# Order of the first operands, unordered scatters, and where the early units' weights lie

## The chip, the cores and the metric

The kernel runs on one core of a Trainium2 chip. The metric is the time of one execution on the device, in microseconds. The core has five engines that run side by side, each through its own instructions in order: TensorE (PE; its weight loads are PEld), VectorE (DVE), ScalarE (ACT), GpSimd (POOL) and SyncE (SP), which here only issues DMAs and loads registers. Sixteen DMA engines move data between the device's memory and the on-chip memory; transfers whose rows are picked by an index list are issued by POOL, nearly all others by SP.

## What is computed

Three layers, all in float32 at the edges. The attention has 4 x 8 heads of 576 positions and 64 columns, with a decay from the running sum of log f:

```python
log_f = np.log(np.clip(f, 0.0001, 1.0)); cum = np.cumsum(log_f, axis=-1)
scores = scale * q @ k.T + cum[:, :, :, None] - cum[:, :, None, :]     # causal
attn_out = softmax(scores) @ v                                         # (4, 8, 576, 64)
x = attn_out.transpose(0, 2, 1, 3).reshape(2304, 512)
# mixture: each token goes to one of 8 experts
logits = x @ w_gate + modality_bias[modality_id]; e = argmax(logits)
x = gate * (relu(x @ w1[e]) @ w2[e])                                   # w1 512x1024, w2 1024x512
# second layer: a rational function between two products
h = x @ w_in; g = P(h) / (Q(h) + 1e-6); out = g @ w_out                # 512x2048, 2048x512
```

## The kernel before, in words

The program is not issued as it is written. `Rec` records every operation with its engine, a cost, the operations that it depends on, a priority (`up`, plus an offset by kind) and extra order edges (`order`); `flush` (line 230) then lists all of them through a model of the engines and issues each engine's instructions in the order found. So nearly every instruction in the profile has line 163, and tiles tell the stages apart. Some order is written by hand: while `line` is set, SP's transfers keep their written order; while `chained` is set, TensorE's do; `gate` holds back all that follows behind one operation.

**Start.** `constants` and `masks` fill constants and the causal masks; `Attention.setup` (line 587) zeroes the operand tiles of all pairs of heads ("ka", "qa", "one" on POOL; "hq", "lq" on DVE) and makes the decay's running sums, which go through memory ("cums") into rows of "ka". Then pairs 0 and 1 are transposed and split into high and low parts (`parts`), pair 0's row maxima are taken (`maxes`, `turned`), the router is set up (`Route.setup`), and the scales of V are computed (`scales`) and applied (`vparts`, on POOL).

**Attention.** 16 pairs of heads, software-pipelined by the string ORDER: in the loop of pair p, TensorE makes maxima for p+1 (M), scores for p (S), values for p-1 (V), router logits for p-2 (L) and transposes for p+2 (T). An exponential leaves ACT in a tile of the ring "pe" (four), ACT casts it to 16 bits, and POOL subtracts to get the low part "lo". "pe" and "lo" lie in the memory "old"; raw Q, K, V and the value scales' input lie in "prep".

**Routing.** After every fourth pair a batch of 576 tokens is routed (`Route.batch`, line 982): the token numbers and gates of each expert are scattered into a table in memory, with five transfers of up to 128 rows. `Route.early` picks two full blocks of 128 tokens from the first two batches; `Route.final` (line 1070) lays out all others after the fourth.

**Units.** A unit is one expert for one block of 128 tokens, or two blocks ("double"). `fetch` (line 1228) reads its part of the table and gathers the tokens; `pieces` (line 1201) brings the expert's weights in 16 pieces of 256 KB, each cast (ACT) and subtracted (DVE) into two parts, through rings of 4 raw and 3 converted tiles. There are two early units, then eight double and seven single ones. The rings lie in the memory of "old", which the program takes over when the attention has left it (`Mixed`), and all eight PSUM banks are likewise taken over after the attention (`banks_of`); an early unit uses four of them, two for products with w1 ("ph") and two for products with w2 ("py").

**Second layer.** `Weights.fill` (line 1151) converts 32 tiles of w_in and w_out from float64 into the memories that the attention has left, gated behind the last of `final`. `Second.tile` (line 1381) then computes nine tiles of 256 tokens and scatters the output rows by token number, two transfers each; the list lays them among the remaining units.

What a scatter waits for is decided in two places: the recorder sees a write to the whole table, and the framework below it adds a wait behind the transfer before, in the table and in the output.

Of the kernel before, what the change touches and what calls it, by code (L numbers as in the profile page):

```python
# [11 lines left out]
P = 128  # L12
# [31 lines left out]
class Rec:  # L44
# [10 lines left out]
    def __init__(s, nc):  # L55
        s.nc, s.ops, s.acc, s.bank, s.up, s.tag, s.memory, s.order, s.pages = nc, [], {}, {}, 0, '', {}, [], {}
        s.chained, s.link = False, None
        s.line, s.tail, s.gate = False, None, None
        for e in s.ENG:
            setattr(s, e, Port(s, e))  # L60
# [65 lines left out]
    def op(s, e, cost, fn, ins=(), outs=(), deps=(), share=1.0):  # L126
# [103 lines left out]
    def flush(s):  # L230
# [31 lines left out]
        for t, i in best[1]:  # L262
            ops[i][2]()

# [282 lines left out]
class Attention:  # L547
# [13 lines left out]
    def __init__(s, nc, ar, f32r, prep, ya, old, banks, dr, q, k, v, f, c):  # L561
# [7 lines left out]
        s.pe, s.lo = old.ring(b["pe"], [P, 2, 512]), old.ring(b["hl"], [P, 2, 1664], F16)  # L569
# [17 lines left out]
    def setup(s, f32r):  # L587
# [6 lines left out]
        for t in s.ka.bufs:  # L594
# [9 lines left out]
        G.memset(s.one.bitcast(F32), 0.0)  # L604
        for h in range(2):
            G.memset(s.one[64 * h + 32:64 * h + 34].bitcast(F32), 1.0)
# [87 lines left out]
    def prep(s, p):  # L694
        s.load(p)
        s.loadv(p)
        s.sums(p)
        s.vparts(p)
# [92 lines left out]
    def scores(s, p, g):  # L791
# [63 lines left out]
class Route:  # L855
# [14 lines left out]
    def load(s):  # L870
# [7 lines left out]
        nc.sync.dma_start(out=s.table.rearrange("(p c) t -> p (c t)", p=P), in_=z)  # L878
# [103 lines left out]
    def batch(s, b):  # L982
# [37 lines left out]
        V.tensor_copy(row, r)  # L1020
        for c in range(NB):
            n = P if c < 4 else 64
            nc.gpsimd.indirect_dma_start(out=s.table, out_offset=bass.IndirectOffsetOnAxis(ap=row[:n, c:c + 1], axis=0), in_=mt[:n, c], in_offset=None)
# [146 lines left out]
class Units:  # L1170
# [57 lines left out]
    def fetch(s, i, rows):  # L1228
# [4 lines left out]
        for h in s.halves(i):  # L1233
            ld, box = s.route.reg(h, 1)
            mt = s.mt.next()
            nc.op("D", 60, lambda mt=mt, box=box: nc.nc.sync.dma_start(out=mt, in_=s.route.table[bass.ds(box[0], P), :]),
                  [s.route.table], [mt], [ld])
# [111 lines left out]
class Second:  # L1349


    def __init__(s, nc, ar, keep, units, w, out, c, pa, po):
# [6 lines left out]
        s.tid = keep.ring(4, [P, 1], I32)  # L1359
# [21 lines left out]
    def tile(s, T, need):  # L1381
# [40 lines left out]
        for po, t in zip(pos, tids):  # L1422
            o = s.ab.next()
            nc.scalar.copy(o, po)
            nc.gpsimd.indirect_dma_start(out=s.out, out_offset=bass.IndirectOffsetOnAxis(ap=t, axis=0), in_=o, in_offset=None)
# [234 lines left out]
```

## Time and profile before

| | us |
|---|---|
| median of 3 runs | 1096.74 |
| range of the runs | 1095.72 to 1100.85 |
| the profiled execution | 1102.44 |
| its span, first to last instruction | 1100.7 |
| TensorE busy in it | 994.6 (90%) |
| DVE, ACT, POOL busy | 824.7, 656.6, 393.3 |

All times of rows are microseconds from the span's start. An instruction's idle time stands in brackets, with what ended it. The busy time of TensorE counts a slow matmul as busy; the granted clock tells where it ran at less than full speed (1.00). By stage: start to 33, attention to 270, early units and routing to 345, units with the second layer's weights to 485, second layer and the rest of the units to the end.

### The profile page before, as it was taken

The page shows a single profiled execution, that of the slowest core. Times are in us where ns is not written, and L with a number is a line of the kernel's source. Part 1 is how long each engine was busy: PE and PEld are TensorE (multiplying, and loading weights), DVE is VectorE, ACT ScalarE, POOL GpSimd, SP SyncE. Part 2 cuts the span into 40 slices and gives each one's busy share as a digit, 9 for nine tenths or more (in the row PEclk, how much of TensorE's full clock was granted, in tenths as well). Part 3 has the DMA queues.
Part 4 walks back from the last instruction along what each step waited for, and adds up shares of the span by engine and source line. Part 5 has one row for each costly group of instructions (what it writes and reads, how often), then busy time and mean ns, then how long its engine had stood idle before and what let it go on. Part 6 is the DMA issues. An engine that isn't in the chain of part 4 may idle for free.

```text
span 1100.7 us, 22578 instructions
## 1 busy us (share of the span) xinstructions
PE 994.6 (90%) x8246; PEld 845.9 (77%) x8246; DVE 824.7 (75%) x1484; ACT 656.6 (60%) x1034; POOL 393.3 (36%) x353
## 2 busy tenths in 40 slices
PE   3899999997667888999999999999999999999995
PEld 2778877886436667778888888888877888888794
DVE  6566768673769988877877778667759879889674
ACT  1466556664456667665564646556567677676572
POOL 7676686855232333321221222212122222111131
PEclk9999999998878999999999999999999999999998
DMA  6544343202867888882010010334254454553300
GB/s 146 156 103 126 89 89 78 57 25 55 221 229 241 277 264 269 278 255 80 3 56 30 11 39 11 103 118 144 94 176 154 128 181 142 171 165 106 124 11 19
DMA packets 157375, 138.27 MB, mean 126 GB/s; under 512 B 73392, under 2 KB 115664, under 8 KB 157264
## 3 DMA queue, kind: packets, MB, share of 16 engines
q1 hardware_dynamic: 152288, 123.63, 38.3%
q0 software_dynamic: 4640, 13.13, 3.6%
q8 instruction: 64, 1.05, 0.4%
q14 instruction: 47, 0.39, 0.1%
q10 hardware_dynamic: 336, 0.08, 0.0%
HBM read 120.38 MB, written 16.33 MB: 124 GB/s over the span
## 4 chain that ended last, share of the span: by engine, by line
PE 53%; DVE 19%; DMA 13%; issue 5%; ACT 5%; POOL 2%; SPq 1%; POOLq 0%; DVEq 0%; ACTq 0%
PE pair L163 36%; PE one L163 11%; DVE y L163 10%; PE pair L742 6%; DMA b<-in_moe_w_dram 6%; DVE b L163 5%; ACT y L163 3%; DVE keep L163 2%; DVE at L163 2%; DMA table<-keep 2%; DMA prep<-in_v_dram 1%; ACT b L163 1%; POOL old L163 1%; DMA ys<-b 1%; DMA y<-in_moe_w_out_dram 1%
## 5 line engine op out<-in xcount | busy, mean ns | idle before, releaser
L163 PE MATMUL pair<-b,b 128*128 128x256 f32 (+1 forms) x1032 | 220.1, 330 | 27.4 <-ACT b L163 13.3
L163 DVE TENSOR_TENSOR b<-b,b 128x512 fp32r<-128x512 f32 x272 | 205.2, 769 | 51.4 <-ACT b L163 29.1
L163 ACT CAST b<-b 128x512 fp32r<-128x512 f32 x272 | 165.4, 618 | 99.7 <-DMA b<-in_moe_w_dram 38.0
L163 POOL TENSOR_TENSOR y<-y,y 128x512 f32<-128x512 f32 x72 | 99.4, 1380 | 316.2 <-ACT y L163 296.4
L163 PEld LDWEIGHTS pair<-b,b 128*128 128x128 f32 x1032 | 165.0, 199 | 57.8 <-DVE b L163 20.4
L163 DVE SCALAR_TENSOR_TENSOR y<-y,keep,y 128x512 f32<-128x512 f32 (+1 forms) x216 | 177.9, 832 | 19.4 <-ACT y L163 11.9
L163 PE MATMUL one<-b,b 128*128 128x512 f32 x552 | 175.4, 407 | 13.0 <-ACT b L163 8.1
L742 PE MATMUL pair<-f32r 64*128 64x288 f32 (+4 forms) x1152 | 123.7, 334 | 12.0 <-DVE at L163 7.0
L163 ACT ACTIVATE y<-y,keep 128x512 f32<-128x512 f32 x144 | 108.6, 768 | 26.4 <-POOL y L163 24.5
L163 PEld LDWEIGHTS one<-b,b 128*128 128x128 f32 x552 | 94.5, 189 | 35.0 <-DVE b L163 12.8
L163 POOL TENSOR_TENSOR old<-old,at 128x960 f16<-128x960 f32 (+1 forms) x64 | 108.7, 1709 | 30.6 <-ACT at L163 30.4
L742 PEld LDWEIGHTS pair<-f32r 64*128 64x128 f32 x1152 | 91.7, 196 | 19.1 <-DVE at L163 9.1
L163 PE MATMUL pair<-f32r,y 128*128 128x512 f32 x378 | 104.7, 398 | 0.0
L163 ACT ACTIVATE old<-pair,keep 128x960 f32<-128x960 f32 (+1 forms) x64 | 59.2, 925 | 70.4 <-PE pair L742 63.4
L163 PE MATMUL pair<-y,f32r 128*128 128x256 f32 x624 | 99.6, 283 | 0.0
L163 PEld LDWEIGHTS pair<-y,f32r 128*128 128x128 f32 x624 | 90.5, 188 | 6.2 <-DVE y L163 0.6
L163 DVE TENSOR_REDUCE at<-pair 128x2 f32<-128x576 f32 (+2 forms) x96 | 65.3, 707 | 34.7 <-PE pair L742 29.3
L163 PE MATMUL pair<-at,y 128*128 128x512 f32 x270 | 79.8, 406 | 5.5 <-DVE y L163 5.5
L163 ACT ACTIVATE y<-y 128x512 f32<-128x512 f32 x104 | 66.9, 644 | 22.1 <-DMA y<-in_moe_w_in_dram 12.5
L163 ACT ACTIVATE y<-pair,keep 128x512 f32<-128x512 f32 x70 | 54.2, 775 | 39.0 <-PE pair L163 21.0
L163 PEld LDWEIGHTS pair<-f32r,y 128*128 128x128 f32 x378 | 67.4, 191 | 11.1
L163 DVE TENSOR_TENSOR y<-y,pair 128x512 f32<-128x512 f32 x70 | 47.7, 682 | 28.0 <-ACT y L163 27.6
(136 smaller groups left out, 1721.7 us busy)
## 6 DMA issues: line engine op xcount, KB each, us to landing
b<-in_moe_w_dram SPq DMA_DIRECT2D x272, 256.0 KB
y<-in_moe_w_in_dram SPq DMA_DIRECT2D x16, 512.0 KB
y<-in_moe_w_out_dram SPq DMA_DIRECT2D x16, 512.0 KB
ys<-b SPq DMA_DIRECT2D x25, 257.0 KB
y<-ys SPq DMA_DIRECT2D x18, 257.0 KB
prep<-in_v_dram SPq DMA_DIRECT2D x4, 1152.0 KB
prep<-in_k_dram SPq DMA_DIRECT2D x32, 128.0 KB
prep<-in_q_dram SPq DMA_DIRECT2D x32, 128.0 KB
```

The lines of the kernel that those rows point to most:

```text
L163: fn = lambda: getattr(getattr(s.nc, eng), name)(*(x() for x in ra), **{n: x() for n, x in rk.items()})
L742: T.matmul(o, lhsT=w, rhs=x, start=st, stop=sp, skip_group_check=True)
```

## The change

Four things. (1) At the start, an operation may be gated per engine (`gates`): on POOL all behind the first pair's "ka", on DVE all behind the decay sums; "one" comes first, "ka" and "qa" are filled pair by pair, the masks' last copies come after `setup`. `Route.setup`, `scales` and the first `vparts` are recorded in pair 0's loop, after S1, and pair 2's V load with them. (2) Table and output scatters no longer wait for each other inside a batch (or at all, for output rows); a scatter of a batch waits for those of the batch before, a table read for the last batch's. Ahead of each goes a memset of a 128x1 tile on POOL. (3) "old" and "prep" change sizes and places: half of the ring "pe" moves to "prep", the last three pairs use the half in "old" alone, and the units' rings take over "prep" instead of "old". (4) From the last pair on the attention uses two of its three double banks; the third is taken over for the early units, which then have one bank for "ph" and one for "py". The other six are taken over after the early units.

```diff
@@ Rec.op
         if s.gate is not None:
             s.order.append((s.gate, i))
+        if e in s.gates:
+            s.order.append((s.gates[e], i))
@@ Rec
+    def behind(s, x, ys):
+        for y in ys:
+            s.tc.add_manual_dep(x, y.name, mybir.DependencyInfo(mybir.DependencyClass.Sync, mybir.DependencyReason.DATA))
@@ Attention
-        s.pe, s.lo = old.ring(b["pe"], [P, 2, 512]), old.ring(b["hl"], [P, 2, 1664], F16)
+        s.pe, s.lo = old.ring(b["pe"] // 2, [P, 2, 512]), old.ring(b["hl"], [P, 2, 1664], F16)
+        s.few, s.pe = s.pe, Ring(prep.ring(b["pe"] // 2, [P, 2, 512]).bufs + s.pe.bufs)
@@ Attention.setup
-        for t in s.ka.bufs:
+        G.memset(s.one.bitcast(F32), 0.0)
+        for h in range(2):
+            G.memset(s.one[64 * h + 32:64 * h + 34].bitcast(F32), 1.0)
+        for t, u in zip(s.ka.bufs, s.qa.bufs):
             G.memset(t.bitcast(F32), 0.0)
...
-        for t in s.qa.bufs:
-            G.memset(t.bitcast(F32), 0.0)
+            nc.gates["G"] = nc.gates.get("G", len(nc.ops) - 1)
+            G.memset(u.bitcast(F32), 0.0)
             for h in range(2):
-                G.memset(t[64 * h + 32:64 * h + 34].bitcast(F32), 1.0)
...
-        for r in (s.hq, s.lq):
-            for t in r.bufs:
-                V.memset(t[:, :, :64].bitcast(F32), 0.0)
-                V.memset(t[:, :, 64 + S:].bitcast(F32), 0.0)
+        nc.gates = {"V": len(nc.ops) - 2}
+        for t in [r.bufs[i] for i in range(3) for r in (s.hq, s.lq)]:
+            V.memset(t[:, :, :64].bitcast(F32), 0.0)
+            V.memset(t[:, :, 64 + S:].bitcast(F32), 0.0)
@@ Attention.scores
             s.Pm[p] = s.hi.next(), s.lo.next()
+            if p == NP - 3:
+                s.pe = s.few
@@ Route.batch
-            nc.gpsimd.indirect_dma_start(out=s.table, ...)
+        before, now = s.now, []
+        def scatter(to, src):
+            nc.nc.gpsimd.memset(s.apart, 0.0)
+            x = nc.nc.gpsimd.indirect_dma_start(out=s.table, ...).ins
+            for y in now:
+                nc.tc.declare_no_dep(x, y, reason="rows of different tokens")
+            nc.behind(x, before)
+            now.append(x)
@@ Units.fetch
+            def read(mt=mt, box=box, now=s.route.now):
+                nc.behind(nc.nc.sync.dma_start(out=mt, in_=s.route.table[bass.ds(box[0], P), :]).ins, now)
+            nc.op("D", 60, read, [s.route.table], [mt], [ld] + s.route.ids)
@@ Second.tile
+            def scatter(o=nc.real(o), t=t):
+                nc.nc.gpsimd.memset(s.apart, 0.0)
+                x = nc.nc.gpsimd.indirect_dma_start(out=s.out, ...).ins
+                for y in s.rows:
+                    nc.tc.declare_no_dep(x, y, reason="rows of different tokens")
+                s.rows.append(x)
@@ program
-        kk, uu, yy, pp, ee, ff = (int(x * KB) for x in (10.5, 36.3125, 32.9375, 28, 12, 52))
+        kk, uu, yy, pp, ee, ff = (int(x * KB) for x in (10.5, 28, 32.9375, 36.3125, 12, 52))
...
-        first = pool("old")
-        old = Arena(first.__enter__(), uu, "old")
+        first = pool("prep")
+        prep = Arena(first.__enter__(), pp, "prep")
...
         at.setup(f32r)
+        mask()
+        nc.gates = {}
...
-        ro.setup()
-        at.scales(0, ro.sw)
-        for p in range(2):
-            at.vparts(p)
+        begin = len(nc.ops) - 1
...
+            if p == NP - 1:
+                banks["t"] = Ring(pairs[:2])
...
-                nc.line = not p
-                at.prep(p + 2)
+                nc.line = p < 2
+                at.prep(p + 2, p > 0)
...
+                if p == 0 and x + g == "S1":
+                    nc.tag, nc.gates = '', {"V": begin, "G": begin}
+                    ro.setup()
+                    nc.gates = {}
+                    at.scales(0, ro.sw)
+                    for j in range(3):
+                        if j == 2:
+                            at.loadv(j)
+                        at.vparts(j)
...
-        un.attach(Mixed(nc, pools, lambda: first.__exit__(None, None, None), old.t))
+        bank = banks_of(nc, pools, tc, psum[1], "right", [whole[2][:, :]])
+        un.attach(Mixed(nc, pools, lambda: first.__exit__(None, None, None), prep.t))
-        un.ph, un.py = Ring(bank[0:2]), Ring(bank[2:4])
+        un.ph, un.py = Ring(bank[:1]), Ring(bank[1:])
...
         wt.fill(en())
-        wt.fill(pn())
         wt.fill(fn())
+        wt.fill(on())
```

## Rows read from the trace of the kernel before

**Rows 1.** Windows: stretch, length, then busy us of PE, PEld, DVE, ACT, POOL; clock, DMA share, GB/s.

```profile
244.00:262.00 18.00, 14.72 (x304) 13.02 (x300) 6.56 (x21) 11.71 (x14) 11.81 (x9) 1.00 0.15 38
270.20:344.50 74.30, 48.92 (x184) 31.74 (x181) 53.04 (x137) 37.13 (x66) 20.66 (x18) 0.79 0.76 226
344.50:460.00 115.50, 102.47 (x587) 84.54 (x587) 103.57 (x157) 77.92 (x137) 40.40 (x30) 0.97 0.84 265
500.00:1080.00 580.00, 563.41 (x3422) 492.13 (x3423) 455.48 (x656) 367.85 (x601) 129.74 (x102) 1.00 0.30 95
```

**Rows 2.** Timeline, 0 to 40 us: start, duration, engine, line, operation [idle before, releaser].

```profile
0.32 0.10 POOL L1638 MEMSET const-float32-0.0<- 128x1 f32 x1 [0.32 <-issue]
...
6.51 1.77 DVE L163 CAST at<-at 64x768 bf16<-64x768 f32 x1 [0.32 <-POOL at L163]
...
17.19 1.32 PE L742 MATMUL pair<-f32r 64*128 64x288 f32 x6 [3.10 <-POOL f32r L163]
...
22.80 0.23 DVE L163 CAST keep<-prep 128x128 bf16<-128x128 f32 x1 [7.20 <-POOL prep L163]
...
28.39 0.59 PE L163 MATMUL one<-prep,at 128*128 128x1 f32 x2 [0.51 <-DVE f32r L163]
...
33.07 1.22 PE L742 MATMUL pair<-f32r 64*128 64x288 f32 x8
```

**Rows 3.** Timeline of POOL, 225 to 275 us: table scatters of batch 2.

```profile
244.56 1.01 POOL L163 DMA_INDIRECT table<-keep  x1 [0.95 <-DVE keep L163]
...
259.93 0.98 POOL L163 DMA_INDIRECT table<-keep  x1 [1.77 <-DMA table<-keep]
...
265.11 0.91 POOL L163 DMA_INDIRECT table<-keep  x1 [0.69 <-DMA table<-keep]
```

**Rows 4.** Tile "prep" from 205 to 262 us; SP's timeline.

```profile
L163 PEld LDWEIGHTS one<-keep,prep x4: 134/138/140, 215.2 to 229.3; 64*128 64x128 f32 x4
...
267.66 1.46 SPq L1236 DMA_DIRECT2D keep<-table  x3
270.55 1.92 SPq L1219 DMA_DIRECT2D b<-in_moe_w_dram  x4
```

**Rows 5.** Timeline of PE: an early unit's first, last and the first double unit's matmuls.

```profile
276.96 1.22 PE L163 MATMUL pair<-b,b 128*128 128x512 f32 x2 [1.45 <-DVE b L163]
...
335.33 7.16 PE L163 MATMUL pair<-b,b 128*128 128x512 f32 x32 [1.34 <-DVE b L163]
344.53 1.77 PE L163 MATMUL pair<-b,b 128*128 128x256 f32 x11 [2.05 <-ACT b L163]
```

**Rows 6.** Timelines of POOL and SP in batch 3; landing times of tile "table".

```profile
280.62 1.01 POOL L163 DMA_INDIRECT table<-keep  x1 [3.60 <-DVE keep L163]
...
293.37 0.35 SPq L163 DMA_DIRECT2D y<-in_moe_w_in_dram  x1
...
306.54 0.91 POOL L163 DMA_INDIRECT table<-keep  x1 [7.91 <-DMA table<-keep]
...
311.59 0.34 SPq L1236 DMA_DIRECT2D keep<-table  x1
...
342.09 0.47 SPq L163 DMA_DIRECT2D y<-in_moe_w_in_dram  x1
...
DMA to landing us min/median/max: 2.5/5.0/8.6
```

**Rows 7.** Timeline of DVE, 155 to 160 us.

```profile
157.37 0.36 DVE L163 TENSOR_SCALAR keep<-keep 128x5 int32<-128x5 int32 x1 [2.71 <-DMA table<-keep]
```

**Rows 8.** Groups by form: operation, shapes, count, busy us, mean ns, idle before.

```profile
L163 DVE SCALAR_TENSOR_TENSOR y<-y 128x512 int32<-128x512 int32 x64 | 49.0, 766 | 1.1
...
L163 DVE TENSOR_SCALAR y<-y 128x512 int32<-128x512 int32 x32 | 16.9, 527 | 13.6 <-ACT y L163 13.4
```

**Rows 9.** Timeline, 1086 to 1101 us: the last scatter.

```profile
1093.16 0.98 POOL L163 DMA_INDIRECT out_dram<-y,keep  x1 [2.52 <-DMA out_dram<-y,keep]
```

**Rows 10.** Waits of ACT, 262 to 345 us: total us, times, longest.

```profile
ACT b L163 <- DMA b<-in_moe_w_dram: 10.3, 10, 2.7
```

More of the change, by code (lines that the diff above doesn't have):

```diff
@@ L599, in setup @@
                 G.memset(t[64 * h + 32:64 * h + 33, 64 + S:].bitcast(F32), -BIG)
[L600 to L601 removed]
+            nc.gates["G"] = nc.gates.get("G", len(nc.ops) - 1)
+            G.memset(u.bitcast(F32), 0.0)
             for h in range(2):
[L603 to L606 removed]
+                G.memset(u[64 * h + 32:64 * h + 34].bitcast(F32), 1.0)
         for t in s.vt.bufs:
@@ L692, in vparts, with prep @@
         G.tensor_tensor(vt[:, :, :D], v, vt[:, :, D:2 * D], op=ALU.subtract)
-    def prep(s, p):
+    def prep(s, p, all=True):
         s.load(p)
-        s.loadv(p)
         s.sums(p)
-        s.vparts(p)
+        if all:
+            s.loadv(p)
+            s.vparts(p)
     def parts(s, p):
@@ L877, in load, with clear @@
         nc.sync.dma_start(out=md[:64, :, 4], in_=mi[:, 512:].rearrange("b p t -> p b t"))
-        nc.sync.dma_start(out=s.table.rearrange("(p c) t -> p (c t)", p=P), in_=z)
+        s.now, s.apart = [], s.t([P, 1], "apart")
+        def clear():
+            s.now_0.append(nc.nc.sync.dma_start(out=s.table.rearrange("(p c) t -> p (c t)", p=P), in_=z).ins)
+        s.now = s.now_0 = []
+        s.ids = [nc.op("D", 412, clear, [z], [s.table])]
     def t(s, shape, name, dt=F32):
@@ L1020, in batch @@
         V.tensor_copy(row, r)
+        before, now = s.now, []
+        def scatter(to, src):
+            nc.nc.gpsimd.memset(s.apart, 0.0)
+            x = nc.nc.gpsimd.indirect_dma_start(out=s.table, out_offset=bass.IndirectOffsetOnAxis(ap=to, axis=0), in_=src, in_offset=None).ins
+            for y in now:
+                nc.tc.declare_no_dep(x, y, reason="rows of different tokens")
+            nc.behind(x, before)
+            now.append(x)
+        ids = []
         for c in range(NB):
             n = P if c < 4 else 64
-            nc.gpsimd.indirect_dma_start(out=s.table, out_offset=bass.IndirectOffsetOnAxis(ap=row[:n, c:c + 1], axis=0), in_=mt[:n, c], in_offset=None)
+            to, src = row[:n, c:c + 1], mt[:n, c]
+            ids.append(nc.op("Q", nc.dma(src), lambda to=to, src=src: scatter(to, src), [to, src], deps=s.ids))
+        s.now, s.ids = now, ids
     def counts(s):
@@ L1358, in __init__ @@
         s.yh, s.yl = ar.new([P, 4, 256], F32R), ar.new([P, 4, 256], F32R)
-        s.tid = keep.ring(4, [P, 1], I32)
+        s.tid, s.apart, s.rows = keep.ring(4, [P, 1], I32), keep.new([P, 1]), []
     def rational(s, pa):
@@ L1496, in program @@
         nc.pool = pool
-        (ya, yn), (ea, en), (prep, pn) = memory(yy, "y"), memory(ee, "e"), memory(pp, "prep")
+        (ya, yn), (ea, en), (old, on) = memory(yy, "y"), memory(ee, "e"), memory(uu, "old")
         (f32r, fn), (ar, an) = memory(ff, "f32r", F32R), memory(int(207.75 * KB) - kk - uu - yy - pp - ee - ff, "at")
-        first = pool("old")
-        old = Arena(first.__enter__(), uu, "old")
+        first = pool("prep")
+        prep = Arena(first.__enter__(), pp, "prep")
         psum = [tc.tile_pool(name=f"ps{i}", bufs=1, space=PSUM, side=("left", "right")[i]) for i in range(2)]
         opened = [r.__enter__() for r in psum]
-        whole = [opened[i // 2].tile([P, 1024], F32, name=f"pair{i}") for i in range(3)] + [opened[1].tile([P, 512], F32, name=f"one{i}") for i in range(2)]
+        whole = [opened[i // 2].tile([P, 1024], F32, name=f"pair{i}") for i in range(3)] + [opened[0].tile([P, 512], F32, name=f"one{i}") for i in range(2)]
         for x in whole:
@@ L1600, in program @@
             i += 1
+        bank = banks_of(nc, pools, tc, psum[0], "left", [whole[x][:, :] for x in (0, 1, 3, 4)]) + bank
+        banks["x"] = Ring(bank[4:6])
         nc.up = u["route"]
```

20 lines of the change are left out of this document (9 added, 11 removed).

## The prediction

> **What bounds the kernel now.** I read the busy time by stretch first [rows 1]. From 500 to 1080 us TensorE is busy 563 of 580 us at the full clock: nothing to win there except by starting it earlier. What is lost lies ahead of it. From 270.2 to 344.5 TensorE is busy 48.9 of 74.3 us at a mean granted clock of 0.79, so a part even of that ran at the lower level (1.2 GHz instead of 2.4). The work in this stretch is two early units. A unit has 48 matmuls of 512 columns; 32 of them back to back took 7.16 us [rows 5], so a unit is 48 x 0.224 = 10.8 us and, with its 12 transposes, about 12.5. Two are 25 us of work in 74: some 49 are lost. From 344.5 to 460 the bound is another one: DVE is busy 103.6 of 115.5 us and the DMA engines 84%, at 265 GB/s, and TensorE has 13 us idle. The start is the next loss, and the end has a small one.
>
> Then the timelines, for who is waited for. **Start** [rows 2]: DVE waits at 6.51 for a mask that POOL still fills, and casts it; the scan of the decay sums stands behind that on DVE. TensorE's first full group of maxima starts at 17.19 after 3.10 us behind a POOL memset. Then DVE is caught for 7.20 us behind a routing constant of POOL, until 22.80, and the reductions that free TensorE's banks stand behind it. The routing set-up and value scales follow from 28.39, and only at 33.07 the steady loop. **Scatters** [rows 3]: the five table scatters of batch 2 go out from 244.56 to 265.11, each behind the landing of the one before, with the attention's subtractions queued behind them on POOL; the table read of the first early unit (SP, 267.66) waits for the last. **Memory** [rows 4]: the early units' first weight load leaves at 270.55, when the attention's last tiles in "old" are read. **Batch 3** [rows 6]: its five scatters go out from 280.62 to 306.54, 26 us, and the next table read is at 311.59. The first double unit's matmul is at 344.53, behind the last of unit 1 [rows 5].
>
> **The change part by part.** The sum is made against the profiled execution: span 1100.7, 1102.44 with what lies around it, 5.7 above the median of 1096.74. I apply the difference to the median.
>
> Start. Taken from ahead of the sums is the mask's wait and cast, 1.8 us from 6.51 on. The POOL order now puts "one" and the first pair's two tiles first, which takes the 3.10 us wait. So the maxima start near 13 instead of 17.2, and DVE reduces at once instead of after 22.80. It needs the same time as before from there to 28.39, 5.6 us, so the row of maxima leaves near 20, and the loop could start near 22, where it started at 33.07: up to 11 us. Against it: the set-up and scales, 4.7 us from 28.39 to 33.07 and largely waits of TensorE on DVE, are moved into pair 0's loop, not removed, and every instruction of them counts there; TensorE's attention order is chained, so its waits for DVE come back, now beside more reductions. SP takes the third pair's V load behind them, and the V parts of pairs 0 to 2 come to POOL together. I take 8; bounds 3 (the V parts become the next limit) and 12 (the set-up's waits hidden as well).
>
> Scatters in the attention. After batch 0 DVE lost 2.71 us waiting for a table scatter [rows 7]; batch 1 delayed POOL without idling TensorE. I take 2, bounds 0 and 5 (batch 1 as much as batch 0). Added is a POOL memset of 128x1 ahead of each of 38 scatters. The nearest row, a memset of 128x1, took 0.10 us [rows 2]: 4 us of POOL, busy 12 of 18 us in the attention's tail [rows 1]; free where it has that slack, 0.5 us a batch where not. Five scatters in a row hold POOL 5 x 1.1 us; the subtraction behind them is late by that once, instead of behind five landings. The new wait for the earlier batch's scatters is for work some 50 us old.
>
> Early units. Three things let them start. Memory: "prep" is last read by the transposes of pair 15 at 229.3 [rows 4], so loads can leave 41 us before 270.55, into a stretch where the DMA engines are 15% busy [rows 1]. PSUM: the third pair of banks goes at the start of the last pair's loop, one loop of some 14 us after those transposes (sixteen loops from 33 to 262), near 244. Table: without chaining, batch 2's scatters go out from 244.6 to 249 and land by 254. So unit 0 can begin near 250, with 7 pieces ready (4 raw, 3 converted) and 25 to come. A piece of 256 KB takes 1.0 us at 265 GB/s [rows 1]; the old pace was 67.6 us from 276.96 to 344.53 for 32 pieces [rows 5], 2.1 each. I take 1.5, between: 250 + 25 x 1.5 = 288 for the last (275 to 303). Batch 3's own chain: the attention's tail loses POOL's waits of 1.77 + 0.69 us [rows 3], so the first scatter is at 278.2; five issues of 1.1 put the last at 282.6; the median landing in this stretch was 5.0 us [rows 6], so 287.6. From the first early unit's table read to its first matmul it took 9.3 us (267.66 to 276.96): 297 for the first matmul of a double unit, behind the last of both early units at 288. That is 48 us before 344.53.
>
> What is given back. Until 342.09 the kernel before had issued nine loads of the second layer's weights (first 293.37) [rows 6] and converted eight; the new one has none by 297. Each costs DVE 0.53 + 2 x 0.77 = 2.06 us [rows 8] and 524 KB at 265 GB/s, 2.0 us. In the stretch where they now fall DVE and DMA are the bound, so 8 x 2.06 = 16 us come back. One bank each for "ph" and "py": an early unit fills ph five times (transposes, two products, two turns), and each time TensorE must wait until the bank is copied out: one operation of 128x512, or two behind each other, 0.6 to 1.4 us by [rows 8]; ten times 6 to 14 us, less what the attention or batch 3's slack covers: 6. The exponentials' ring of two in the last three pairs makes one wait for POOL's subtraction two tiles back instead of four: under 1 us a pair, hidden by ACT's idle time there (11.7 of 18 us busy, [rows 1]). The middle: 48 - 16 - 6 = 26; bounds 10 (the banks' 14, both early units' last at 303) and 48 (nothing back).
>
> A rule on scatters beside weight loads. The trace shows table transfers landing in 2.5 to 8.6 us [rows 6]. The Trainium skill, "DMA: Bandwidth & Descriptors", section "Queues, rings and completion order", says that each DMA engine takes turns between the queue rows, a packet at a time; by it a scatter in flight beside loads is slow whether chained or not, and overlapping them pays that only once. At 8.6 instead of 5.0 the double units would start 3.6 us later; the trace's spread agrees with the rule.
>
> End. The last scatter, at 1093.16, waited 2.52 us for the landing of the one before [rows 9]. Unchained it goes out behind its own copy and memset: 2 us, bounds 2 and 2.5. The other eight pairs unblock POOL in a stage bound by TensorE: nothing.
>
> Sum: 8 + 2 + 26 + 2 = 38. 1096.7 - 38 = 1059.
>
> **The rivals.** (a) Nothing comes back: the list puts more double units ahead of the second layer, and the eight conversions hide beside them. 8 + 2 + 48 + 2 = 60, to 12 + 5 + 48 + 2 = 67: 1030 to 1037. For it: TensorE has only 13 us idle from 344.5 to 460; against it: DVE at 90%. (b) The early units do not start early, because the order by priority leaves them behind the attention's chained work, and only memory and scatters are won: unit 0 near 262 instead of 277, 15 us, less 4 tiles x 2 = 8. Then 8 + 2 + 7 + 2 = 19, with bounds of the rest 12 to 26: 1071 to 1085. Against it: TensorE is idle 3.3 us of 18 from 244 to 262, and the last pair has no next maxima to compute. (c) Slower: the weight pieces stop the attention. Their casts stand in order on ACT, their subtractions on DVE, their loads on SP ahead of the row copies that scores wait for. From 262 to 345 ACT waited for a piece's load 10 times, 1.03 us each, 2.7 at most [rows 10]. With 25 pieces beside the attention's last 26 us that is 26 us at the mean and 67 at the worst; from 38 / 25 = 1.5 us a piece, all on TensorE's path, the change is lost: 1097 to 1126. Against it: DMA is nearly idle there, so loads land soon.
>
> **How the numbers follow.** Forecast (gain 28 to 55, 1042 to 1069): 0.52. (a) and beyond: 0.13. (b), or the start hidden as well (gain 6 to 28): 0.25. No change within 0.5% (5.5 us, about what a measurement can tell): 0.05. (c): 0.05. Faster 0.90, same 0.05, slower 0.05. The range runs from near the lower end of (a) to the weaker half of (b): 1036 to 1082 leaves out about 0.07 below and 0.13 above.
>
> **What would show it.** The steady loop from about 24 instead of 33; a first early weight load near 222; table scatters in groups of five about 1.1 us apart; the first matmul of a double unit near 289 (297 less the start's 8); the clock no longer down near 270; DVE over 90% from there until the second layer's first tile; the last scatter right behind its copy. It is wrong if unit 0 still begins after the attention, if ACT waits for weight loads inside pairs 14 and 15, or if the second layer's first tile does not move although the double units start earlier.

## The result, and the profile after

| | before | after |
|---|---|---|
| median on one chip (4 runs each), us | 1097.53 | 1084.51 |
| range, us | 1095.72 to 1100.85 | 1083.56 to 1085.45 |
| the profiled execution, its span | 1102.44, 1100.7 | 1083.69, 1081.8 |
| TensorE busy in it | 994.6 | 995.8 |

The ratio is 0.9861, with a 95% interval from 0.9822 to 0.9900: the change gains 13 us, where the forecast was 38 and its range ended at 1082. The profiled execution of before is 4.9 above its median here, so the 18.9 us between the two spans overstate the gain.

The windows of the changed kernel, by stage (busy us of PE, PEld, DVE, ACT, POOL; then clock, DMA share, GB/s):

```profile
230.00:262.00 32.00, 28.57 (x411) 24.73 (x409) 21.16 (x48) 16.65 (x23) 17.00 (x17) 0.73 0.23 72
262.00:344.50 82.50, 64.96 (x486) 48.65 (x485) 57.11 (x152) 44.62 (x75) 23.97 (x25) 0.88 0.68 196
344.50:500.00 155.50, 137.01 (x805) 115.81 (x804) 138.00 (x210) 104.58 (x183) 50.68 (x39) 0.97 0.86 268
500.00:600.00 100.00, 94.08 (x614) 84.10 (x613) 72.18 (x105) 58.00 (x91) 23.37 (x20) 1.00 0.25 73
600.00:1000.00 400.00, 394.53 (x2376) 343.60 (x2375) 324.98 (x475) 264.32 (x437) 97.89 (x86) 1.00 0.34 107
```

TensorE is busy about 995 us in both, so nearly all of the gain is what it idles less: 106.1 us in the span of before and 86.0 in that of after. Idle is a stretch less its busy time. Each line of this table is worked out so from the windows of one profiled execution (the last stretch ends with the span); it comes back below for the experiments.

| TensorE idle, us | to 230 | 230-262 | 262-344.5 | 344.5-500 | 500-600 | 600-1000 | to the end |
|---|---|---|---|---|---|---|---|
| before | 28.5 | 4.2 | 27.5 | 18.2 | 2.8 | 12.9 | 12.2 |
| after | 24.7 | 3.4 | 17.5 | 18.5 | 5.9 | 5.5 | 10.5 |

Two stretches carry it, 10 us where the early units run and 7.4 in the second layer, which the forecast had put at nothing. The 3.8 us less to 230 are no gain: the attention has come equally far by then (pair 15's split on DVE, below, is at 230.16 and 230.36), and TensorE was busy 3.9 us longer for it, at a granted clock of 0.97 where before has 0.99. The window of before for the second of the two stretches:

```profile
600.00:1000.00 400.00, 387.15 (x2343) 337.61 (x2342) 314.43 (x457) 258.03 (x428) 88.21 (x71) 1.00 0.37 117
```

**The early units**, in the timelines of SP, POOL and PE (start, duration, engine, line, operation, [idle before, releaser]):

```profile
229.58 2.22 SPq L1248 DMA_DIRECT2D b<-in_moe_w_dram  x4
...
263.11 1.46 SPq L1266 DMA_DIRECT2D keep<-table  x3
...
247.27 1.02 POOL L1042 DMA_INDIRECT table<-keep  x1 [2.96 <-DVE keep L165]
...
256.76 0.90 POOL L1042 DMA_INDIRECT table<-keep  x1 [0.19 <-issue]
...
265.31 0.99 POOL L165 DMA_INDIRECT keep<-xnat,keep  x1 [0.15 <-PE pair L753]
...
271.65 3.01 PE L165 MATMUL pair<-b,b 128*128 128x512 f32 x12
...
324.85 1.04 PE L165 MATMUL one<-b,b 128*128 128x256 f32 x7
```

The first weights leave at 229.58 (270.55 in [rows 4]), 7.6 us later than the 222 foreseen but 41 earlier than before; yet unit 0 begins at 271.65, only 5.3 us earlier than in [rows 5]: it waits for its tokens, whose scatters end at 256.76, whose table read is at 263.11 and whose gathers follow from 265.31. The first double unit comes 19.7 us earlier (344.53 in [rows 5]). The second layer's first tile is read later, in SP's timelines of after and of before:

```profile
507.67 0.34 SPq L1419 DMA_DIRECT2D y<-ys  x1
```

```profile
482.08 0.34 SPq L1389 DMA_DIRECT2D y<-ys  x1
```

**A stall ahead of that**, in the timelines of DVE, POOL and PE:

```profile
239.57 0.68 DVE L165 TENSOR_TENSOR b<-b,b 128x512 fp32r<-128x512 f32 x1
...
240.35 0.68 DVE L165 TENSOR_TENSOR b<-b,b 128x512 fp32r<-128x512 f32 x1
...
241.29 1.79 DVE L165 CAST keep<-keep 128x40 bf16<-128x40 f32 x1
...
241.04 3.23 POOL L165 TENSOR_TENSOR old<-old,at 128x960 f16<-128x960 f32 x2 [2.90 <-ACT at L165]
...
243.13 0.39 PE L165 MATMUL one<-keep 128*128 128x40 bf16 x10 [2.50 <-DVE keep L165]
```

These two subtractions of early weights, and one more at 233.72, stand among batch 2's small operations; the cast behind them falls beside POOL's subtraction and takes 1.79 us (in before, ahead of POOL's, 0.17), and TensorE waits 2.50 us for the batch's products. What follows, as a window:

```profile
244.00:262.00 18.00, 17.54 (x214) 15.35 (x214) 7.59 (x23) 7.21 (x8) 10.55 (x14) 0.54 0.09 23
```

Its granted clock is 0.54 there, nearly all of it at the lower level (1.2 GHz of 2.4), where it was 1.00 in [rows 1], and the first part of pair 15's values is written at 272.76 instead of 266.69, the second at 281.34 instead of 270.93. This is one execution: behind the same wait, of 2.48 to 2.50 us, the three others of this kernel have 0.91, 0.82 and 0.81.

**Batch 3 and the end**, from POOL's timeline, against [rows 6] and [rows 9]:

```profile
292.77 1.21 POOL L1042 DMA_INDIRECT table<-keep  x1 [20.50 <-DVE keep L165]
...
298.12 0.91 POOL L1042 DMA_INDIRECT table<-keep  x1 [0.19 <-issue]
...
1072.90 1.01 POOL L1457 DMA_INDIRECT out_dram<-y,keep  x1 [8.12 <-ACT y L165]
1073.92 0.11 POOL L1456 MEMSET keep<- 128x1 f32 x1
1074.22 0.96 POOL L1457 DMA_INDIRECT out_dram<-y,keep  x1 [0.19 <-issue]
```

Five scatters in 5.4 us where they took 26, but the first is 12 us later than in before: the attention's tail, which they need, is late too, its last router logits at 284.08 where before has them at 273.64. Batch 2's five (above) are not so close, since a subtraction of POOL stands between the third and the fourth. The last output row goes out behind its own memset, without the 2.52 us.

**The start**: the first rows of the steady loop, the set-up and scales in it, and the transposes' split on DVE of pairs 2 and 15:

```profile
19.46 1.22 PE L753 MATMUL pair<-f32r 64*128 64x288 f32 x8
...
25.68 0.67 PE L753 MATMUL pair<-f32r 64*128 64x192 f32 x2 [4.12 <-DMA f32r<-f32r]
...
30.34 0.58 PE L165 MATMUL one<-prep,at 128*128 128x1 f32 x2
...
35.02 0.85 PE L753 MATMUL pair<-f32r 64*128 64x288 f32 x4
...
39.80 1.23 DVE L165 TENSOR_TENSOR f32r<-pair,f32r 128x1024 fp32r<-128x1024 f32 x1 [1.80 <-ACT f32r L165]
...
230.16 1.23 DVE L165 TENSOR_TENSOR f32r<-pair,f32r 128x1024 fp32r<-128x1024 f32 x1 [1.21 <-ACT f32r L165]
```

And of before, the third group of the loop and the same two splits:

```profile
35.33 1.31 PE L742 MATMUL pair<-f32r 64*128 64x288 f32 x8
...
43.52 1.23 DVE L163 TENSOR_TENSOR f32r<-pair,f32r 128x1024 fp32r<-128x1024 f32 x1 [1.77 <-ACT f32r L163]
...
230.36 1.22 DVE L163 TENSOR_TENSOR f32r<-pair,f32r 128x1024 fp32r<-128x1024 f32 x1 [1.21 <-ACT f32r L163]
```

The loop's first group of matmuls comes at 19.46, 13.6 us earlier than the same group in [rows 2] (33.07). The second is then held up for 4.12 us by a row copy that before has behind it by then, and the third begins at 26.12, 9.2 us ahead of before. The set-up and scales take 4.68 us inside the loop, from 30.34 to 35.02, as they took ahead of it (28.39 to 33.07). At pair 2 the lead is 3.7 us, at pair 15 0.2.

### The profile page after: what moved, and what is told of

Read it like the earlier page. It is cut to its first block, busy times and chain, and to the rows that moved or that the text cites. A ratio compares the mean times of both kernels' runs of the same rounds, so it can differ in the third digit from the quotient of the medians.

```text
span 1081.8 us, 22653 instructions
## 1 busy us (share of the span) xinstructions
PE 995.8 (92%) x8246; PEld 851.6 (79%) x8246; DVE 825.5 (76%) x1484; ACT 657.0 (61%) x1034; POOL 402.4 (37%) x391
## 4 chain that ended last, share of the span: by engine, by line
PE 58%; DVE 18%; DMA 10%; issue 5%; ACT 5%; POOL 2%; SPq 1%; DVEq 0%; ACTq 0%; POOLq 0%
PE pair L165 38%; PE one L165 12%; PE pair L753 8%; DVE y L165 8%; DVE b L165 6%; DMA b<-in_moe_w_dram 5%; ACT y L165 3%; ACT b L165 2%; DVE keep L165 2%; DVE at L165 2%; DMA y<-in_moe_w_in_dram 1%; DMA y<-in_moe_w_out_dram 1%; DMA keep<-xnat,keep 1%; DMA f32r<-f32r 1%; SPq L165 1%
## 5 line engine op out<-in xcount | busy, mean ns | idle before, releaser
L165 PE MATMUL pair<-b,b 128*128 128x512 f32 x648 | 207.9, 420 | 27.2 <-ACT b L165 16.5
L165 DVE SCALAR_TENSOR_TENSOR y<-y,keep,y 128x512 f32<-128x512 f32 (+1 forms) x216 | 173.2, 811 | 18.6 <-ACT y L165 10.5
L165 PE MATMUL one<-b,b 128*128 128x256 f32 (+1 forms) x936 | 173.7, 309 | 9.8 <-ACT b L165 8.3
L165 PEld LDWEIGHTS pair<-b,b 128*128 128x128 f32 x648 | 116.2, 196 | 58.9 <-ACT b L165 23.0
L165 PEld LDWEIGHTS one<-b,b 128*128 128x128 f32 x936 | 140.4, 194 | 27.0 <-ACT b L165 11.8
L165 PE MATMUL pair<-f32r,y 128*128 128x512 f32 x432 | 122.4, 396 | 1.5 <-DVE y L165 1.4
L165 DVE TENSOR_REDUCE at<-pair 128x2 f32<-128x576 f32 (+1 forms) x96 | 65.4, 706 | 39.8 <-PE pair L753 36.1
L165 POOL TENSOR_TENSOR old<-old,at 128x1024 f16<-128x1024 f32 (+3 forms) x38 | 66.0, 1751 | 34.5 <-ACT at L165 34.4
L165 PE MATMUL pair<-y,f32r 128*128 128x256 f32 x528 | 76.6, 283 | 1.2 <-DVE y L165 1.2
L165 PEld LDWEIGHTS pair<-y,f32r 128*128 128x128 f32 x528 | 71.0, 188 | 4.2 <-DVE y L165 2.2
L165 POOL DMA_INDIRECT keep<-xnat,keep x32 | 36.9, 1153 | 81.9 <-DMA keep<-table 29.8
```

The lines of the kernel that those rows point to most:

```text
L165: fn = lambda: getattr(getattr(s.nc, eng), name)(*(x() for x in ra), **{n: x() for n, x in rk.items()})
```

## The experiments

The kernel before takes 1097.5 to 1109.7 us on the chips used, the changed one 1082 to 1086, so ratios are compared within one comparison alone. All are against the kernel before, with 95% intervals. Comparisons 1 and 4 hold no run of the changed kernel; a kernel of theirs can only be set against what it has in the others, 0.9782 to 0.9861.

| comparison | kernel | median, us | ratio |
|---|---|---|---|
| 1 | undo_memory | 1086.12 | 0.9861 (0.9828 to 0.9893) |
| 1 | undo_scatters | 1102.99 | 1.0001 (0.9976 to 1.0026) |
| 1 | undo_start | 1081.71 | 0.9812 (0.9771 to 0.9853) |
| 1 | subs_late | 1079.73 | 0.9806 (0.9766 to 0.9847) |
| 2 | after_again | 1085.76 | 0.9782 (0.9738 to 0.9827) |
| 2 | list_kept | 1121.05 | 1.0130 (1.0081 to 1.0179) |
| 2 | order_old | 1106.53 | 0.9963 (0.9930 to 0.9995) |
| 2 | out_ordered | 1093.08 | 0.9864 (0.9821 to 0.9906) |
| 3 | after_third | 1082.11 | 0.9857 (0.9813 to 0.9900) |
| 3 | scat_first | 1083.07 | 0.9874 (0.9826 to 0.9922) |
| 3 | both_moved | 1085.09 | 0.9876 (0.9830 to 0.9921) |
| 3 | start_old_moved | 1081.42 | 0.9837 (0.9792 to 0.9883) |
| 4 | scatters_alone | 1089.85 | 0.9899 (0.9879 to 0.9919) |
| 4 | memory_alone | 1109.91 | 1.0079 (1.0053 to 1.0105) |
| 4 | start_alone | 1103.42 | 1.0013 (0.9989 to 1.0037) |
| 4 | table_ordered | 1088.35 | 0.9881 (0.9861 to 0.9902) |
| 5 | after_fourth | 1084.64 | 0.9858 (0.9826 to 0.9890) |
| 5 | undo_memory_2 | 1087.02 | 0.9891 (0.9863 to 0.9918) |

And where TensorE idled in each that the text uses. Each line is one execution; in the four of the changed kernel a value moves by up to 3 us, from 600 to 1000 by 0.2.

| TensorE idle, us | to 230 | 230-262 | 262-344.5 | 344.5-500 | 500-600 | 600-1000 | to the end |
|---|---|---|---|---|---|---|---|
| undo_memory | 24.0 | 4.9 | 22.1 | 21.6 | 1.6 | 5.1 | 10.5 |
| undo_scatters | 21.7 | 5.1 | 29.1 | 18.2 | 4.2 | 13.3 | 11.9 |
| undo_start | 28.8 | 5.0 | 17.5 | 17.7 | 2.0 | 7.8 | 10.0 |
| list_kept | 27.1 | 3.1 | 29.9 | 24.2 | 7.2 | 9.9 | 12.9 |
| order_old | 22.6 | 4.1 | 30.2 | 20.8 | 3.8 | 13.7 | 11.0 |
| out_ordered | 24.0 | 4.9 | 19.6 | 17.9 | 2.5 | 12.8 | 11.8 |
| table_ordered | 24.4 | 5.0 | 31.0 | 19.3 | 1.8 | 7.0 | 10.4 |
| scatters_alone | 30.9 | 3.9 | 20.4 | 18.1 | 3.1 | 10.9 | 11.2 |
| memory_alone | 30.7 | 4.8 | 25.4 | 18.7 | 3.9 | 15.2 | 13.1 |
| start_alone | 25.6 | 1.4 | 25.9 | 17.7 | 2.8 | 15.5 | 13.2 |
| after_fourth | 23.4 | 6.3 | 17.4 | 21.1 | 5.1 | 5.5 | 10.5 |
| undo_memory_2 | 25.7 | 4.6 | 25.8 | 20.1 | 1.4 | 5.0 | 10.4 |

### One part undone

Parts (3) and (4) undone, and then each of the others; the list of instructions is written anew in each case:

```diff
@@ undo_memory
-        (old, on) = memory(yy, "y"), memory(ee, "e"), memory(uu, "old")
+        (prep, pn) = memory(yy, "y"), memory(ee, "e"), memory(pp, "prep")
-        un.ph, un.py = Ring(bank[:1]), Ring(bank[1:])
+        un.ph, un.py = Ring(bank[0:2]), Ring(bank[2:4])
@@ undo_scatters (table and output)
-            nc.op("Q", nc.dma(o), scatter, [o, t])
+            nc.gpsimd.indirect_dma_start(out=s.out, ...)
@@ undo_start
-        mask()
-        nc.gates = {}
```

> The changed kernel with the early units' weights back in the attention's old memory and the banks released together, as in the kernel before; the first operands' order and the unordered scatters stay. Theory A (the early units' move gives next to nothing, because unit 0 waits for its tokens and the end of the attention pays for the early loads): within 4 us of the changed kernel, 1081 to 1088, first double unit's matmul between 320 and 335, first tile of the second layer near 485. Rival B (the move of the weights carries the 13 us): 1094 to 1098.

> The changed kernel with the table's and the output's scatters each waiting for the one before again. Theory A (the last batch's scatters, 5.4 us where they took 26, bring the first double unit forward, and the end adds 2): 1093 to 1097, most of the 13 us gone, first double unit near 340. Rival B: 1086 to 1088, only the end's 2.3 us and little of the middle lost.

> The changed kernel with the first operands, the masks and the routing constants in the order of the kernel before. Theory A (the 7 us that the loop starts earlier are gone by pair 15, 230.16 against 230.36): 1083 to 1086. Rival C (the start is carried to the end): 1091 to 1092.

Theory A came out on all three by the ratio: without the move of the weights about all of the gain is there (0.9861), without the start's order too (0.9812), without the scatters nothing (1.0001). Its times and dates did less well. undo_scatters, at 1102.99, lost all of the gain where most was foreseen; undo_start, at 1081.71, is below its range; and in undo_memory the first double unit is at 336.81 (foreseen 320 to 335) and the second layer's first tile is read at 502.90 (near 485).

### One part alone

```diff
@@ scatters_alone: before, with part (2)
@@ memory_alone: before, with parts (3) and (4)
@@ start_alone: before, with part (1)
```

> The kernel before with the unordered scatters of both kinds as its only change. If they carry the whole gain (undoing them left nothing of it, undoing either other part left all of it): a ratio to the kernel before of 0.982 to 0.988. If the parts only work together, the early units' weights being what the free scatters are worth: 0.992 to 1.000.

> The kernel before with the early units' weights in the memory that is left early, and the banks split for them, as its only change. If the move is worth nothing by itself (the tokens of the third batch are then still scattered one after the other, until 265 and beyond): 0.997 to 1.003. The forecast's own sum for it was 26 us: 0.976.

> The kernel before with the first operands' new order as its only change. If the lead is lost in the attention: 0.998 to 1.002. If it is carried: 0.993.

The scatters alone give 11 us, a ratio between the two ranges foreseen. The move of the weights alone costs 8.7, outside of what was expected, and the start 1.4, within the noise. So alone the parts come to 1 us, and together to 13: they do not add up. The PE timeline of memory_alone and POOL's show two things that the move brings:

```profile
246.69 0.39 PE L165 MATMUL one<-keep 128*128 128x40 bf16 x10 [2.50 <-DVE keep L165]
...
272.04 0.91 POOL L165 DMA_INDIRECT table<-keep  x1 [1.85 <-DMA xnat<-y]
277.24 0.98 POOL L165 DMA_INDIRECT keep<-xnat,keep  x1 [4.29 <-DMA keep<-table]
```

The early weights bring the same stall of 2.50 us into the attention, and their tokens are not in the table before the last of five chained scatters, at 272.04: unit 0 begins at 283.11, 6 us later than before. Where the 8.7 us go is not shown by this: the idle from 262 to 344.5 even falls by 2 us, to 25.4, and more idle stands to 230 (2.2) and from 600 to 1000 (2.3), in a list that was written anew. Whether the move is worth anything beside free scatters, on one chip:

> The changed kernel as it is, beside the one without the move of the weights: 1082 to 1087.

> The changed kernel with the early units' weights and the banks as in the kernel before, on the same chip as the changed kernel. If the move, which costs 8.7 us by itself, is worth nothing even where the table's scatters are free: within 2 us of the changed kernel, or faster. If the free scatters are what it needs: 3 to 8 us slower than the changed kernel.

The move is worth 2.4 us there, by overlapping intervals no more than a hint. The idle table says where the rest of it goes: 8.4 us are won from 262 to 344.5 (25.8 to 17.4), and 3.7 are lost again from 500 to 600, at the start of the second layer, whose first tile is read at 508.59 with the move and at 503.13 without it. Another 2.7 are lost from 230 to 262 and from 344.5 to 500.

### The waits, or the order written for them

```diff
@@ list_kept: the changed kernel's list, the waits back
-            for y in now:
-                nc.tc.declare_no_dep(x, y, reason="rows of different tokens")
...
-                for y in s.rows:
-                    nc.tc.declare_no_dep(x, y, reason="rows of different tokens")
@@ order_old: the waits gone, the list as in undo_scatters
-            nc.op("Q", nc.dma(o), scatter, [o, t])
+            nc.op("Q", nc.dma(o), scatter, [o, t], [s.out])
```

> The changed kernel as it is, timed beside the three others of this comparison: 1084 to 1090, where the kernel before is at 1098 to 1103, a ratio near 0.986.

> The changed kernel, its written order of instructions unchanged, with each scatter waiting again for the one before (the two declarations of independence are left out). Theory E (the waits themselves cost the time: the last batch's five scatters over some 20 us again, and 18 output scatters in chains): 1095 to 1103, back at the kernel before. Rival F (the gain lies in the order that is written when no landing stands between two scatters, and not in the waits): 1086 to 1091, the end's 2.3 us and little else lost, and TensorE's waits in 600 to 1000 stay near 5 us.

> The reverse: the instructions in the order that is written when the scatters count as ordered (the same list, instruction for instruction, as with both kinds of scatter undone), but at run time no scatter waits for another. Theory E (the waits): 1084 to 1089. Rival F (the order): 1097 to 1103, TensorE idle some 13 us in 600 to 1000 as with the scatters undone.

By the idle time rival F came out on order_old, and neither theory on list_kept, which is slower than both allow: the gain needs the new list and the free scatters together. By their traces DVE and ACT run the same instructions in the same order in list_kept as in the changed kernel, and in order_old as in undo_scatters. The list written for free scatters loses 35 us when the waits come back (1121.05 against 1085.76), 11 more than the kernel before: POOL's scatters stand next to each other in its list, with the attention's subtractions behind them; POOL waits for landings, ACT for POOL, and TensorE for ACT. This is one stretch; the rest of the 35 us was not followed. The waits of that kernel from 230 to 300 us (total, times, longest), and its PE timeline:

```profile
POOL table L1042 <- DMA table<-keep: 8.1, 3, 3.1
...
PE pair L753 <- ACT old L165: 6.7, 1, 6.7
...
ACT old L165 <- POOL keep L1041: 5.7, 1, 5.7
...
276.72 1.86 PE L753 MATMUL pair<-f32r 64*128 64x448 f32 x8 [6.70 <-ACT old L165]
```

The reverse, the old list without the waits, gets 3 us of the 24 that the change is worth on this chip. From 600 to 1000 TensorE idles 13.7 us, as with the waits (13.3). PE's largest waits there (total, times, longest) in the kernel before, in order_old, and in the changed kernel:

```profile
PE pair L163 <- DVE y L163: 4.4, 5, 1.5
PE pair L163 <- DVE b L163: 2.7, 3, 1.6
```

```profile
PE pair L165 <- DVE y L165: 6.8, 8, 1.5
PE pair L165 <- ACT y L165: 2.7, 1, 2.7
```

```profile
PE pair L165 <- DVE b L165: 2.6, 4, 1.6
PE pair L165 <- DVE y L165: 1.8, 3, 0.8
```

So the second layer's gain is not the scatters' waiting time alone: without the waits the old list keeps all of the idle time, and with them the new one still has less of it (9.9, though in a kernel that is some 30 us late there). In all, TensorE waits there 9.6 us for DVE, 3.3 for ACT and 1.4 for a DMA in order_old, and 4.4, 0.5 and nothing in the changed kernel, behind lists in which DVE and ACT run in another order. Which placement does it was not isolated.

### Table or output

```diff
@@ out_ordered: output scatters recorded and chained as before
@@ table_ordered: table scatters recorded and chained as before
```

> Only the output rows' scatters ordered again, the table's stay free. If the second layer holds most of it (TensorE idle 13.3 us in 600 to 1000 with all scatters undone, 5.5 in the changed kernel, and 2.3 at the end): 1093 to 1098. If the last batch's table holds it (its scatters 5.4 us where they took 26): 1086 to 1089.

> The changed kernel with only the table's scatters ordered again, the output's free. With the output's ordered again and the table's free the ratio was 0.986 where the changed kernel's was 0.978. If the two kinds share the gain: this one also loses some 8 us of it, 0.986 to 0.992 on a chip where the changed kernel has 0.978 to 0.986. If the table's part was the lesser: within 3 us of the changed kernel.

Both share it. With the output ordered 8 us are lost, and the idle from 600 to 1000 is back at 12.8. With the table ordered the idle there stays at 7.0, and that from 262 to 344.5 is back at 31.0, though the early weights still lie in "prep". On the two chips' different scales, the table's part can't be told closer than 2 to 11 us.

Since every edit has the list written anew, a lucky list is a rival to any one of these results. For the output's scatters the runs taken together speak against it. Every kernel whose list was written for ordered output scatters idles 12.8 to 15.5 us from 600 to 1000 (before, undo_scatters, order_old, out_ordered, memory_alone, start_alone), every one written for free ones 5.0 to 10.9. The spread inside the second group shows what else the list can do: scatters_alone has 10.9 and undo_memory, which differs from it only by the order at the start, 5.1.

### The stall, and unit 0's start

```diff
@@ subs_late (Rec.flush): three subtractions of early weights and the loads behind them
+        for x, y in [(3358, 2818), (3335, 2818), (3352, 2818), (3329, 2818), (3346, 2818), (3323, 2818)]:
+            line.remove(x)
+            line.insert(line.index(y) + 1, x)
@@ scat_first: batch 2's last scatters, then the early table reads
+        for x, y in [(2823, 2821), (2822, 2821), (3442, 2823), (3312, 2823), (3309, 2823)]:
@@ both_moved: both; start_old_moved: both, on undo_start
```

> The changed kernel with one edit in the written order: VectorE's three subtractions of the first early unit's weights, and the loads that take their place, come after the third batch's row numbers instead of among its small operations (they started at 233.72, 239.57 and 240.35). Theory A (they and the stretched cast at 241.29 made TensorE wait 2.50 us for the batch's products, and it then ran at 0.50 of its clock from 244 to 261): no wait over 1 us at those products, granted clock of 1.00 from 244 to 261, values of pair 15 near 267 instead of 272.76, total 1076 to 1081. Rival D (the clock falls there anyway, in 246 to 262, as it did at 264 to 281 before): 1083 to 1086.

> The changed kernel as it is, beside the three others of this comparison: 1083 to 1087.

> The changed kernel with one edit in the written order: the third batch's last two scatters stand ahead of GpSimd's subtraction (which waited 2.33 us at 253.16), and the early units' three table reads ahead of the attention's store of pair 13 on the transfer queue. Unit 0's first matmul should come at 258 to 264 instead of 271.65. If the early units' late start costs the time: 1077 to 1081. If TensorE is full with the attention until 272 anyway (it was busy 17.54 of 18 us in 244 to 262, at 0.54 of its clock): 1083 to 1087.

> Both edits of the written order, the subtractions late and the scatters and reads first. Unit 0's first matmul at 255 to 262 and no long wait of TensorE before 244. If both delays cost time and add up: 1072 to 1077. If only the attention's stall costs: 1077 to 1081, as with the subtractions alone.

> Both edits of the written order, and the first operands in the order of the kernel before. If the earlier start is worth nothing at the end (its lead of 3.7 us at pair 2 was 0.2 at pair 15): the same as both edits with the new start, within 3 us. If it is carried where the rest does not swallow it: 6 to 8 us slower than that.

In comparison 3 none differs from the changed kernel clear of the intervals; both_moved, at 1085.09, is slower than both of its ranges, and start_old_moved is 3.7 us faster than it, where at most 3 us of difference, or a loss, had been foreseen. subs_late, at 1079.73, lies in the range of theory A, but no changed kernel was timed beside it, its ratio of 0.9806 lies inside the changed kernel's 0.9782 to 0.9861, and its clock from 244 to 262 is 0.81, not 1.00. So it is not shown that the attention's stall costs time, nor that it costs none: what the edits took away came back elsewhere. In subs_late TensorE waits 2.67 us for a row copy at 249.83. In both_moved the batch's products wait no more, but the attention does, for such a row copy, which stands behind the moved weight loads on SP's queue (PE, then SP):

```profile
254.95 0.91 PE L759 MATMUL pair<-f32r 64*128 64x192 f32 x2 [3.81 <-DMA f32r<-f32r]
...
246.49 1.57 SPq L1254 DMA_DIRECT2D b<-in_moe_w_dram  x3
248.65 1.43 SPq L165 DMA_DIRECT2D f32r<-f32r  x2
```

In scat_first the scatters end at 251.04 and the table read is at 255.84, 7.3 us earlier, and yet the gather and unit 0 (271.80, where 258 to 264 was foreseen) do not move, since the attention's subtractions stand ahead of the gather on POOL:

```profile
255.84 1.42 SPq L1272 DMA_DIRECT2D keep<-table  x3
...
260.78 2.01 POOL L165 TENSOR_TENSOR old<-old,at 128x960 f16<-128x960 f32 x1 [4.32 <-ACT at L165]
264.06 1.28 POOL L165 TENSOR_TENSOR old<-old,at 128x576 f16<-128x576 f32 x1 [1.28 <-ACT at L165]
265.50 0.99 POOL L165 DMA_INDIRECT keep<-xnat,keep  x1 [0.15 <-PE pair L759]
```

## Why the prediction was wrong

**The sign and the end were right.** The end's 2 us are there, and the scatters of batch 3 go out about 1.3 us apart (1.1). But of the signs named, the first double unit is at 324.85 (near 289 foreseen), DVE is busy 69% from 262 to 344.5 and 89% from 344.5 to 500 (over 90%), and the clock rose from 0.77 to 0.88 from 262 to 344.5 and fell from 1.00 to 0.73 from 230 to 262. None of the three signs of being wrong is there: unit 0 begins inside the attention's last pair, ACT waits for no weight load in pairs 14 and 15, and the second layer's first tile did move, the wrong way.

**Start: 8 forecast, nothing measured.** The first operands come as early as foreseen and more: the loop begins at 19.46. Three steps behind that failed. The second group of the loop waits 4.12 us for a row copy, which in before passed behind the set-up; the set-up and scales cost in the loop what they cost ahead of it, 4.68, named in the forecast but not taken off in full; and the 3.7 us left at pair 2 were taken to last. 1.9 of them go between pairs 3 and 4, where the granted clock is 0.88 from 47 to 75 us (1.00 in before), and 3.8 (out of a lead of 3.2) between pairs 8 and 9, behind a TensorE wait of 1.68 us for DVE at 129.82, with a clock of 0.79 from 132 to 146 (1.00 in before). Why the clock fell there is not shown. Alone the part measures 1.0013.

**Early units: 26 forecast; the move of the weights measured 2.4 (alone: a loss of 8.7).** The 26 also held the free scatters of batch 3, so the two figures do not cover the same thing; the idle of TensorE from 262 to 344.5, which both act on, fell by 10 us. This term failed, at four of its steps. First, "unit 0 can begin near 250" stands ahead of its own "land by 254": with the 9.3 us from the table read to the first matmul the forecast's figures give 263, and the list's order on POOL and SP made it 271.65. Second, batch 3's first scatter was put at 278.2, as if the early units cost the attention's tail nothing; it went out at 292.77, behind a tail that had run at a clock of 0.73 from 230 to 262 (1.00 in before). The one landing of this batch that the trace gives took 8.9 us, where the sum had 5.0. Third, "48 us before 344.53" turned the date of one marker into a gain. What could be won in the stretch from 262 to 344.5 was what TensorE idles there, 27.5 us in all, plus what its clock costs; the double units did come 19.7 us earlier and the idle fell by 10. In table_ordered they come at 346.52, later than before, and that kernel still has a ratio of 0.9881. Fourth, the give-back of 16 us of DVE between 344.5 and 500 is not there (18.5 us idle against 18.2). What is there is the second layer's first tile, read at 507.67 instead of 482.08, and 3.1 us more idle from 500 to 600. Most of that delay comes with the free table scatters, not with the early units: with the scatters alone the first tile is at 503.97, with the move alone at 482.06, and with the move and an ordered table at 477.87. Why it does was not followed. The 6 us for single banks were not tested by themselves.

**Scatters: 2 in the attention and 2 at the end forecast, some 11 measured alone.** By the idle time of scatters_alone, 7.1 us of them lie from 262 to 344.5, which the forecast had counted inside its 26. "The other eight pairs unblock POOL in a stage bound by TensorE: nothing" is the sentence that failed: from 600 to 1000 TensorE was idle 12.9 us, nearly all of it in 14 waits of up to 1.7 us, 8.4 us of them for DVE; it is idle 10.9 there with the scatters alone and 5.5 in the changed kernel. I had read "busy 563 of 580" [rows 1] as full and did not ask what the remaining 17 were. That the list is written by a model to which the chain of landings is a cost, so that dropping the chain rewrites the order far from any scatter, was in the code and not in my sum.

**The rivals.** The time fell at the edge of (b), 1071 to 1085, and its core held nearly: unit 0 starts only 5.3 us early (15 in (b)). Its reason held in part, for it is POOL's and SP's written order, and not TensorE's chain alone. (c), slower, is what the move of the weights does by itself, but not in the way foreseen: ACT waits for no weight load in the attention's last pairs. A stall behind the subtractions on DVE is there instead; that it makes the loss is not shown. (a) is out.

## What to carry to other kernels

Price a change in what the bounding engine idles, or runs slowly, in each stretch, and take no more from a stretch than stands there; the earlier date of one operation is no gain by itself. Where a program orders its instructions by a model, a dropped dependency acts through the new order, everywhere: try it with the old order and with the old waits before saying which of the two pays, and look at the same stretch over several lists before crediting one edit. And a resource that comes free earlier is worth nothing, or less, while another input of the same work comes late.

## What the runs showed of the hardware

A small cast on DVE, 128x40 float32 to bfloat16, takes 0.17 to 0.18 us alone, and 1.79 us when it starts 0.25 us behind POOL's subtraction of 128x960; one to int32 of 128x5, at 124.33, took 1.06 instead of 0.17, 0.36 us behind the start of a subtraction of POOL that takes 1.36. The first cast ends at 243.08; a subtraction of that size took 2.02 us elsewhere in this trace, so POOL's ends at 243.06, by that estimate. The second cast ends at 125.39, POOL's subtraction at 125.33. The Trainium skill, "SBUF — State Buffer", section "Who interferes with whom", has DVE's casts in their two-port mode and POOL share one pair of ports as a lock that the first to start holds for its whole instruction; the trace agrees in these two places, and no run here varied it by itself.

A TensorE wait of 2.50 us in the attention was followed by a mean granted clock of 0.54 from 244 to 262 us in one execution; behind the same wait of 2.50 us another execution of the same kernel (after_third) has 0.82 there, so what followed the wait differed from run to run.

The kernel before differs by 1% from chip to chip (medians of 1097.5 to 1109.7 us), the changed one by 0.3%.
